# Part of a layer norm's statistics moved from DVE to Pool, and the last tile's tail in halves, in a two-layer linear-attention kernel

## The chip, the cores and the metric

The kernel runs on one core of a Trainium2 chip. The metric is the device time of one execution in microseconds (us), and lower is better. Times are medians of several executions, with the lowest and the highest in brackets. A profile is one execution of its own and its span is about 1.7 us shorter than the execution's time (392.7 against 394.39 us for the kernel before).

The engines are PE (matrix multiplication), PEld (PE's weight loads, which overlap its matmuls), DVE (vector), ACT (scalar), POOL (GpSimd) and SP (which only issues transfers here).

## The reference

Two equal layers, each of a linear attention block and a gated MLP, both behind a layer norm and with a residual. Here x is 1 x 2048 x 512, there are 32 heads of 16, F is 1376 and everything is bf16.

```python
def _layernorm(x, axis=-1, eps=1e-5):
    m = jnp.mean(x, axis=axis, keepdims=True)
    v = jnp.var(x, axis=axis, keepdims=True)
    return (x - m) / jnp.sqrt(v + eps)

def _A_ref(x, wqkv, w_phi, wo):            # shortened
    q, k, v = split_heads(x @ wqkv)
    pq, pk = q @ w_phi, k @ w_phi           # for each head
    phi_q = concat([softmax(pq), softmax(-pq)])
    phi_k = concat([softmax(pk), softmax(-pk)])
    kv, z = sum_s(phi_k outer v), sum_s(phi_k)
    return merge_heads(phi_q @ kv / (phi_q @ z + 1e-6)) @ wo

def _B_ref(x, W_gate, W_up, W_down):       # shortened
    gate = x @ W_gate
    return (relu(gate) * (x @ W_up)) @ W_down

x = x + _A_ref(_layernorm(x), ...);  x = x + _B_ref(_layernorm(x), ...)
x = x + _A_ref(_layernorm(x), ...);  x = x + _B_ref(_layernorm(x), ...)
```

## The kernel before

The sequence is cut into 16 tiles of 128 rows. The kernel isn't written as streams of instructions. It records operations, each with an engine, the resources that it reads and writes, and a duration from a table. A list scheduler then chooses one order for all of them. It runs forward and backward passes over modelled start times, replays each order found with durations varied by up to 8%, and keeps the order with the shortest modelled span. The order is then emitted as one in-order stream per engine, with semaphores for the dependences.

```python
class Program:                                            # cut
    def schedule(self):
        ...
        noise = [[rng.uniform(0.92, 1.08) for _ in ops] for _ in range(self.TRIALS)]
        best = None
        for weight in self.ORDER_WEIGHTS:                 # 4 weights
            prio = [weight * o.idx - rank[o.idx] - o.boost for o in ops]
            for _ in range(self.PASSES):                  # 12 passes
                start, finish, order = self._forward(prio)
                span = self._replay(order, noise)
                if best is None or span < best[0]:
                    best = (span, start, finish, order)
                prio = [t - o.boost for t, o in zip(self._backward(start, finish), ops)]

    def _forward(self, prio):
        ...
            if o.is_dma:
                q_free = max(st + self.DMA_FIXED * 0.35, q_free) + o.dma_bytes / self.DMA_BW
                finish[i] = q_free + self.DMA_FIXED * 0.65
            else:
                finish[i] = st + o.dur
```

The first layer norm ("L0") runs its statistics in batches of four tiles. For tiles 4 to 15 the odd tiles are applied on ACT, the even ones on DVE, and a DMA transposes each result for PE:

```python
    def ln_stats(self, ts, tag):
        ...
        for t in ts:
            op("dve", bn_stats(stats6[t] <- x_sb[t]), 685, f"{tag} stats {t}")         # two halves: count, mean, count x variance
            op("dve", bn_aggr(mv[t] <- stats6[t]),    172, f"{tag} aggr {t}")          # mean, variance
        op("pool", tensor_scalar(rv1[t0:t1] <- mv[..., 1:2] + EPS_LN), 225 + 4 * n, f"{tag} rv1 {t0}")
        op("pool", tensor_tensor(rstd[t0:t1] <- rv1 pow mhalf),        550 + 20 * n, f"{tag} rstd {t0}")

    def ln(self, t, tag, on_act=False, ...):
        ...
        if on_act:
            op("pool", nmr[t] <- mv[t, 0] * rstd[t] * -1.0, 280, f"{tag} nmr {t}")
            op("act", activation(ytile <- x_sb[t], Identity, scale=rstd[t], bias=nmr[t]), 825, f"{tag} apply {t}")
        else:
            op("dve", tensor_scalar(ytile <- (x_sb[t] - mv[t, 0]) * rstd[t]), 407, f"{tag} apply {t}")
        ...
        self.dma_tr(yT[:, :, t * 128:(t + 1) * 128] <- ytile, f"{tag} tr {t}")
```

These are shortened: the lambdas and resource lists are left out. In the same stage, the keys of the attention are normalised: a sum on DVE ("Zk"), a reciprocal on DVE ("rZk") and a multiplication of 128 x 1024 on Pool ("phik"), for tiles 14 and 15 half on Pool and half on DVE.

The tail is the down projection of tile 15 in the last MLP, its residual add and its store:

```python
    def glu_down(self, t, ring, tag):
        bank = next(ring)
        for fc in range(NFC):                                       # 11 matmuls of 512 columns
            op("pe", matmul(pb[bank] += hT[fc].T @ Wd[fc]), 216, f"{tag} down {t} {fc}")
        op("dve", x_sb[t] <- x_sb[t] + pb[bank], 685, f"{tag} resid {t}")

    def store(self, t):
        self.dma("sp", out[t] <- x_sb[t], ..., 131072, f"store {t}")
```

The softmax here doesn't subtract the row's maximum and nothing guards it: scores larger than these inputs give would overflow.

## Time and profile before

| | before |
|---|---|
| time | 394.07 us (393.86 to 394.39, 3 runs) |
| span of the profile | 392.7 us |
| PE busy | 377.3 us (96%), 2277 matmul records for 2320 weight loads |
| PE clock granted | full in every slice |
| last key normalisation on Pool ends | 53.2 us |

First come lines of the profile page of the kernel before: the busy times (in brackets the share of the span, then the number of instructions), and the shares by engine of the chain of work that ended last.

```profile
PE 377.3 (96%) x2277; PEld 206.9 (53%) x2320; DVE 267.4 (68%) x554; ACT 207.1 (53%) x389; POOL 166.4 (42%) x272
...
PE 84%; DVE 5%; POOL 4%; DMA 2%; ACT 2%; issue 2%; SPq 0%; DVEq 0%; ACTq 0%; POOLq 0%
```

PE bounds the kernel. Note the two counts: each matmul of this kernel has a weight load of its own, so 43 matmul records are missing from this trace.

Next is the table by stretches of the kernel before (some stretches are left out): start and end, then sum and mean of the stretch's length, then the busy time of each engine with the number of instructions.

```profile
core 0: us, PE busy (x) PEld busy (x) DVE busy (x) ACT busy (x) POOL busy (x), PEclk, DMA share, GB/s
10.00:20.00 10.00, 8.93 (x49) 4.47 (x49) 9.67 (x28) 8.43 (x16) 3.60 (x8) 1.00 0.83 211
20.00:30.00 10.00, 8.83 (x65) 4.94 (x65) 10.00 (x14) 9.73 (x14) 8.89 (x8) 1.00 0.38 73
30.00:40.00 10.00, 9.62 (x61) 5.01 (x62) 9.36 (x13) 8.08 (x11) 10.00 (x6) 1.00 0.40 80
80.00:240.00 160.00, 159.11 (x921) 84.92 (x935) 117.55 (x225) 70.00 (x138) 71.56 (x109) 1.00 0.17 33
262.00:280.00 18.00, 16.80 (x131) 12.34 (x133) 14.36 (x40) 9.52 (x27) 9.37 (x23) 1.00 0.29 60
```

From 10 to 40 us DVE and ACT are busy 80% of the time or more, Pool nearly all of it from 20 us on, and PE has gaps. In the middle PE is nearly full. But read 80 to 240 us with the counts: there are 921 matmuls for 935 loads, and fourteen missing matmuls account for the missing 0.9 us. The gap in 262 to 280 us, of 1.2 us, is another matter, since only two records are missing there.

Two more views of the kernel before, by time (start, duration, engine, line, operation, output<-inputs; in square brackets the idle time before it and what ended it), show the stage that the change edits. DVE:

```profile
21.45 2.04 DVE L564 TENSOR_SCALAR ytile<-x_sb,mv,rstd 128x512 bf16<-128x512 bf16 x1
23.41 0.54 DVE L601 RECIPROCAL rZk<-Zk 128x64 f32<-128x64 f32 x1
```

Pool:

```profile
21.42 1.93 POOL L604 TENSOR_TENSOR expk<-expk,rZk 128x1024 bf16<-128x1024 bf16 x1
...
24.11 1.93 POOL L604 TENSOR_TENSOR expk<-expk,rZk 128x1024 bf16<-128x1024 bf16 x1 [0.17 <-DVE rZk L601]
26.69 1.94 POOL L604 TENSOR_TENSOR expk<-expk,rZk 128x1024 bf16<-128x1024 bf16 x1 [0.65 <-DVE rZk L601]
```

The DVE apply at 21.45 (tile 6) lasted 2.04 us instead of about 0.4: it lay over the whole of Pool's first normalisation. That pushed the reciprocal behind it to 23.41, and Pool then twice waited for reciprocals.

The tail of the kernel before, on DVE:

```profile
388.83 0.69 DVE L754 TENSOR_TENSOR x_sb<-x_sb,ps 128x512 bf16<-128x512 bf16 x1 [3.29 <-PE ps L752]
389.69 0.69 DVE L754 TENSOR_TENSOR x_sb<-x_sb,ps 128x512 bf16<-128x512 bf16 x1 [0.18 <-PE ps L752]
```

### The profile page before, as it was taken

Reading aid. Unit: us, or ns where it says so; the run is one execution under the profiler, and the core shown is the slowest. Engines: PE = TensorE matmul, PEld = TensorE weight load, DVE = VectorE, ACT = ScalarE, POOL = GpSimd, SP = SyncE. Lnnn points to the kernel's source line nnn. Section 1 sums busy time; section 2 is a strip of 40 time slices with the busy share of each in tenths; the row PEclk is TensorE's granted clock in tenths of the full one; section 3 lists DMA queues with packets and bytes.
Section 4 is the critical chain, followed back from the end, with each engine's and each line's share of the span. In section 5 each row is a group of like instructions: output and inputs, shape, how many; then the busy total and the mean of one; then the engine's idle time right before and its main releaser. Section 6 shows DMA issues by size and latency. Waiting matters only on the chain.

```text
span 392.7 us, 6311 instructions
## 1 busy us (share of the span) xinstructions
PE 377.3 (96%) x2277; PEld 206.9 (53%) x2320; DVE 267.4 (68%) x554; ACT 207.1 (53%) x389; POOL 166.4 (42%) x272
## 2 busy tenths in 40 slices
PE   5889999999999999999999999989999999999996
PEld 3445564677644444444444467467774454444442
DVE  4999878777757899857747867877875666222122
ACT  5898659744624413532553484975564462453350
POOL 5389945642623463363334552574444253000000
PEclk9999999999999999999999999999999999999999
DMA  6833672322211322401000110242323132100001
GB/s 182 220 69 79 200 276 43 67 53 43 42 40 27 43 53 46 85 7 29 13 13 2 27 29 2 48 61 53 76 54 61 27 56 53 42 14 13 15 27 53
DMA packets 61519, 23.01 MB, mean 59 GB/s; under 512 B 53456, under 2 KB 60464, under 8 KB 61488
## 3 DMA queue, kind: packets, MB, share of 16 engines
q1 hardware_dynamic: 60912, 22.08, 24.8%
q10 hardware_dynamic: 576, 0.52, 0.5%
q8 instruction: 18, 0.29, 0.3%
q14 instruction: 13, 0.11, 0.1%
HBM read 7.91 MB, written 2.10 MB: 25 GB/s over the span
## 4 chain that ended last, share of the span: by engine, by line
PE 84%; DVE 5%; POOL 4%; DMA 2%; ACT 2%; issue 2%; SPq 0%; DVEq 0%; ACTq 0%; POOLq 0%
PE ps L728 39%; PE ps L752 19%; PE ps L587 7%; PE ps L707 6%; PE ps L660 5%; PE ps L676 4%; POOL expk L604 3%; DVE stats L547 2%; PE ps L633 2%; PE ps L618 2%; DMA yT<-ytile 1%; DMA x_sb<-in_A_x_dram 1%; POOL rstd L552 1%; DVE ytile L564 1%; ACT expq L663 1%
## 5 line engine op out<-in xcount | busy, mean ns | idle before, releaser
L728 PE MATMUL ps<-yT,Wg 128*128 128x512 bf16 (+3 forms) x435 | 125.9, 336 | 2.0 <-ACT numbf L366 1.1
L728 PE MATMUL ps<-yT,Wu 128*128 128x512 bf16 (+3 forms) x436 | 124.2, 336 | 0.4
L730 ACT ACTIVATE gate_sb<-ps 128x512 bf16<-128x512 f32 (+3 forms) x110 | 56.2, 512 | 108.7 <-PE ps L728 103.2
L752 PE MATMUL ps<-Wd,hT 128*128 128x512 bf16 (+1 forms) x340 | 104.0, 379 | 0.6
L604 POOL TENSOR_TENSOR expk<-expk,rZk 128x1024 bf16<-128x1024 bf16 (+1 forms) x32 | 59.6, 1878 | 30.9 <-DVE rZk L601 21.6
L728 PEld LDWEIGHTS ps<-yT,Wg 128*128 128x128 bf16 (+1 forms) x440 | 43.7, 100 | 34.4 <-issue 1.5
L728 PEld LDWEIGHTS ps<-yT,Wu 128*128 128x128 bf16 (+1 forms) x440 | 43.7, 100 | 33.4 <-ACT expk L735 0.8
L752 PEld LDWEIGHTS ps<-Wd,hT 128*128 128x128 bf16 (+1 forms) x352 | 34.1, 98 | 37.3 <-DVE x_sb L754 0.7
L737 DVE TENSOR_TENSOR hT<-gate_sb,expk 128x512 bf16<-128x512 bf16 (+3 forms) x73 | 28.7, 393 | 31.0 <-ACT expk L735 30.2
L547 DVE BATCH_NORM_STATS2 stats<-x_sb 128x6 f32<-128x512 bf16 x64 | 42.1, 675 | 5.0 <-DMA x_sb<-in_A_x_dram 4.7
L599 DVE TENSOR_REDUCE Zk<-expk 128x64 f32<-128x1024 bf16 x32 | 38.0, 1197 | 10.1 <-ACT expk L590 8.4
L366 ACT ACTIVATE numbf<-ps 128x432 bf16<-128x432 f32 x64 | 32.9, 538 | 17.7 <-PE ps L676 17.4
L701 POOL TENSOR_TENSOR osb<-tsc 128x512 bf16<-128x512 bf16 x28 | 32.7, 1168 | 21.3 <-DVE tsc L696 18.2
L707 PE MATMUL ps<-wo_p,oT 128*128 128x512 bf16 x122 | 38.7, 379 | 0.2
L551 POOL TENSOR_SCALAR rv<-mv 128x1 f32<-128x1 f32 (+1 forms) x55 | 12.3, 229 | 61.0 <-DVE mv L548 60.8
L735 ACT ACTIVATE expk<-ps 128x512 bf16<-128x512 f32 (+3 forms) x73 | 36.2, 495 | 0.6 <-PE ps L728 0.4
L754 DVE TENSOR_TENSOR x_sb<-x_sb,ps 128x512 bf16<-128x512 bf16 x32 | 21.7, 682 | 20.8 <-PE ps L752 20.6
L663 ACT ACTIVATE expq<-ps 128x1024 bf16<-128x1024 f32 (+1 forms) x40 | 32.3, 865 | 6.1 <-PE ps L660 5.8
L676 PE MATMUL ps<-kvbd,expq 128*128 128x144 bf16 x256 | 34.6, 226 | 0.4 <-DVE kvbd L649 0.2
L660 PE MATMUL ps<-yT,Wqp 128*128 128x512 bf16 x121 | 33.6, 379 | 1.2 <-ACT expq L663 1.0
L740 DVE TENSOR_TENSOR hT<-gate_sb,ps 128x512 bf16<-128x512 bf16 (+2 forms) x37 | 22.6, 612 | 17.7 <-PE ps L728 15.7
L552 POOL TENSOR_TENSOR rstd<-rv,mhalf 128x1 f32<-128x1 f32 (+1 forms) x55 | 33.1, 607 | 3.1
(62 smaller groups left out, 428.9 us busy)
## 6 DMA issues: line engine op xcount, KB each, us to landing
out_dram<-x_sb SPq DMA_DIRECT2D x16, 128.0 KB, 1.7
x_sb<-in_A_x_dram SPq DMA_DIRECT2D x3, 512.0 KB, 6.2
Wg<-in_B_W_gate_dram SPq DMA_DIRECT2D x4, 344.0 KB, 4.2
Wu<-in_B_W_up_dram SPq DMA_DIRECT2D x4, 344.0 KB, 6.6
Wd<-in_B_W_down_dram SPq DMA_DIRECT2D x5, 256.0 KB, 7.3
yT<-ytile SPq DMA_TRANSPOSE x60, 2.4
hT<-in_A_wqkv_dram ACTq DMA_DIRECT2D x4, 128.0 KB, 3.2
x_sb<-in_A_x_dram SPq DMA_DIRECT2D x4, 128.0 KB, 3.8
```

The costliest lines, as they stand in the source:

```text
L547: op("dve", (lambda t: lambda e: e.bn_stats(k.stats6[:, t, :], k.x_sb[:, t, :]))(t), [r("x", t)], [r("st", t)], 685, f"{tag} stats {t}")
L552: op("pool", lambda e: e.tensor_tensor(k.rstd[:, t0:t1, :], k.rv1[:, t0:t1, :], k.mhalf[:, 0:n], ALU.pow), [r("rv1", t) for t in ts] + [r( ...
L599: op("dve", lambda e: e.tensor_reduce(k.Zk[:, zb, :], k.expk[:, t, :, :].rearrange("p s (h f) -> p (s h) f", f=16), AX.X, ALU.add), [r("ex ...
L604: op(eng, (lambda s0, s1: lambda e: e.tensor_tensor(k.expk[:, t, s0:s1, :].rearrange("p s (h f) -> p (s h) f", f=16), k.expk[:, t, s0:s1, ...
L660: op("pe", (lambda c, ic, bank: lambda e: e.matmul(k.pb[bank][:], k.Wqp[:, ic, c * 128:(c + 1) * 128], k.yT[:, ic, st * 512:(st + 1) * 512 ...
L663: op("act", (lambda c0, s, b0: lambda e: e.activation(k.expq[:, st, c0:c0 + w, s, :], k.ps[:, b0:b0 + w, :], ACT.Exp, scale=(1.0 - 2.0 * s ...
L676: op("pe", (lambda s, c, j, g0, bank: lambda e: e.matmul(k.pb[bank][:, j * GW:(j + 1) * GW], k.expq[:, st, c, s, tt * 128:(tt + 1) * 128], ...
L707: op("pe", (lambda c, bank: lambda e: e.matmul(k.pb[bank][:], k.oT[:, ob, c, :], k.wo_p[:, c, :], start=(c == 0), stop=(c == NC - 1)))(c, ...
L728: op("pe", (lambda bank, W, ic, fc, Mf: lambda e: e.matmul(k.pb[bank][0:Mf, 0:n], W[:, ic, fc * 128:fc * 128 + Mf], k.yT[:, ic, c0:c0 + n] ...
L730: op("act", (lambda Mf, gb, gs: lambda e: e.activation(k.gate_sb[0:Mf, gs, 0:n], k.pb[gb][0:Mf, 0:n], ACT.Relu))(Mf, gb, gs), [self.RP[gb] ...
L735: op("act", (lambda Mf, ub, tu: lambda e: e.activation(k.expk[0:Mf, tu, 0, 0:n], k.pb[ub][0:Mf, 0:n], ACT.Copy))(Mf, ub, tu), [self.RP[ub] ...
L752: op("pe", (lambda fc, Kf, u, c0: lambda e: e.matmul(k.pb[bank][:], k.hT[0:Kf, u, c0:c0 + 128], k.Wd[0:Kf, fc, :], start=(fc == 0), stop=( ...
```

## The change

The intent has two parts. First, the mean and variance of tiles 8 to 15 of the first layer norm are no longer aggregated on DVE, tile by tile. Pool merges the half statistics of four tiles at once with small operations, and makes the bias for four tiles in one. All applies of tiles 4 to 15 then have the form x * rstd + bias. Second, the down projection of the very last tile is done in two halves of 256 columns, so that only half of the residual add and half of the store follow the last matmul.

```diff
@@ ln_stats (cut)
-            op("dve", ... bn_aggr ..., 172, f"{tag} aggr {t}")
+            if tag != "L0" or ts[0] < 8:
+                op("dve", ... bn_aggr ..., 172, f"{tag} aggr {t}")
+        if tag == "L0" and ts[0] >= 8:
+            return self.aggr_pool(ts, tag)
@@ new (resource lists cut; d = 225 + 4 * n)
+    def aggr_pool(self, ts, tag):
+        op("pool", df <- s6[:, :, 0, 1:2] - s6[:, :, 1, 1:2], d, f"{tag} agdif {t0}")
+        op("pool", sm <- s6[:, :, 0, 1:3] + s6[:, :, 1, 1:3], d, f"{tag} agsum {t0}")
+        op("pool", df <- df * df, d, f"{tag} agsq {t0}")
+        op("pool", sm <- sm * [-0.5, 1 / D], d, f"{tag} agmul {t0}")
+        op("pool", df <- df * 0.25 + EPS_LN, d, f"{tag} agv {t0}")
+        op("pool", rv1 <- df + sm[1], d, f"{tag} rv1 {t0}")
+        op("pool", rstd <- rv1 pow mhalf, 550 + 20 * n, f"{tag} rstd {t0}")
+        op("pool", nmr <- sm[0] * rstd, d, f"{tag} nmr {t0}")
@@ ln (cut)
+        if tag == "L0" and t > 3:
+            if t < 8:
+                op("pool", nmr[t] <- mv[t, 0] * rstd[t] * -1.0, 280, f"{tag} nmr {t}")
+            ...                  # DVE: x * rstd + nmr, 407; ACT as before, 825
@@ glu_down (cut)
-               ..., 216, f"{tag} down {t} {fc}")
+    def glu_down(self, t, ring, tag, halves=1):
+        w = 512 // halves
+        for m in range(halves):
+            bank = next(ring)
+            ...                  # matmul into pb[bank][:, m0:m1] from Wd[:, fc, m0:m1]
+               ..., 0.42 * w + 1, f"{tag} down {t} {fc}")
+            ...                  # residual of the half, 150 + 1.045 * w
@@ store (cut)
+        for m in range(halves):
+            self.dma("sp" if m == 0 else "act", ..., 131072 // halves, f"store {t}")
@@ steps_B
-                    out.append(lambda t=t: self.glu_down(t, dring, B))
+                    out.append(lambda t=t: self.glu_down(t, dring, B, 1 + (last and t == NT - 1)))
```

One side effect: the table's durations of all full down projections turn from 216 to 216.04 and of their residual adds from 685 to 685.04.

## The prediction

> **What bounds the kernel now.** TensorE. On the page PE is busy 377.3 of 392.7 us (96%), and the chain of waits is 84% PE. The table by stretches puts the missing PE time at the two ends: idle 4.4 us in 0–10 us, 1.1 in 10–20, 1.2 in 20–30, 0.4 in 30–40, 0.05 in 40–50, 1.15 in 50–60, about 0.8 in 60–80, and 3.1 in the last 14.7 us. From 80 to 378 us it idles only some 3.3 us of 298. So the change, which touches only the first layer norm (until about 36 us) and the last tile, can move the time by one or two microseconds at most; a gain of 2% (7.9 us) isn't there to be had.
>
> **First layer norm.** Between 10 and 36 us DVE is 94–100% busy and carries the chain (statistics, aggregation, reciprocal, apply), which ends in a wait of PE for a transposed tile at 31 us. The change takes eight aggregations off DVE. One lasts 172 ns, but four in a row add only 0.28 us to the chain, so DVE gains about 0.56 us, not the 1.4 us that the durations suggest. The applies stay on their engines (309–412 ns on DVE).
>
> Pool gets six small operations (0.23–0.24 us each, with 0.07 us between dependent ones) in place of one before each power (1.03 us), and one batched bias operation in place of two; tiles 4 to 7 get two biases more (0.27 us each). That is about +1.4 us of Pool per batch, and each batch's applies can start some 1.5 us later, since all of them now wait for the bias. Batch 8–11 can use Pool idle time (2.6 us before 17.47, 0.67 before 20.11). Batch 12–15 can't: Pool runs the key normalisations from 21.42 to 53.25 us with about 1.2 us idle, and their end releases the last accumulation at 53.3. Unless the scheduler puts a normalisation earlier, that end moves back by about 1 us. The whole order is computed anew, so this may be avoided: the reciprocal that the first normalisation needs ran at 19.93, though its sum was done at 14.2.
>
> One DVE apply took 2.04 us instead of 0.41: it lies wholly over Pool's first normalisation (21.42–23.35). The Trainium skill, "SBUF — State Buffer", section "Who interferes with whom", says that DVE in a two-port mode and GpSimd hold the shared port pair exclusively, so one blocks the other for a whole instruction. The trace agrees with that, and it is 1.6 us on the chain; a shifted order can remove or repeat it.
>
> Net for this part: −0.4 us, uncertain by 1.3.
>
> **Tail.** The last residual add (0.69 us) and then a 1.7 us store follow the last matmul alone. In halves the exposed add is about 0.42 us, with the store of half the bytes on another queue: −0.3 us. PE's down time shouldn't grow: 256-wide matmuls in the page's gate/up groups go at 0.109 us each, half of 0.216.
>
> **Prediction.** 393.4 us, 8 in 10 between 391.9 and 395.1. Faster by over 2%: 0.01; within 2%: 0.98; slower by over 2%: 0.01.
>
> **What would show it.** Right: the aggregation line falls from 64 to 56 executions; DVE's statistics of tiles 8–15 run back to back; about 16 small Pool operations appear before 24 us; from the last matmul to the end it is 0.3 us shorter; PE busy unchanged; the last key normalisation ends within 1.5 us of 53.25. Wrong: that end moved by more than 2 us, or PE idle time between 80 and 378 us changed by over 1 us.
>
> **What would make it wrong.** The recomputed order changing the PE-bound middle; more or fewer DVE applies blocked by Pool; Pool's normalisations starting much earlier or later; half-row stores landing more slowly.

## The result, and the profile after

The kernel after takes 391.80 us (391.07 to 392.33, 4 runs), against 394.23 us (393.86 to 394.43, 4 runs) for the kernel before. The ratio is 0.9938, with a 95% interval from 0.9919 to 0.9957. Here and below, ratios are the mean time of one kernel's runs over that of the other's in the same rounds, so they are not quite the ratio of the medians quoted. The gain is real: the change was measured three times in all, at 0.9938, 0.9939 and 0.9949.

The page of the kernel after, the lines that answer to those of before:

```profile
PE 379.4 (97%) x2331; PEld 208.0 (53%) x2331; DVE 272.0 (70%) x547; ACT 206.6 (53%) x389; POOL 168.5 (43%) x284
...
PE 88%; POOL 4%; ACT 3%; DMA 2%; DVE 1%; issue 1%; ACTq 0%; POOLq 0%
```

This trace is complete: 2331 matmuls and 2331 loads, the 11 more being the halves. So PE's busy time, 379.4 against 377.3 us, says nothing of more work; most of the difference is the 43 missing records. What did move is DVE's share of the chain, from 5% to 1%.

The table by stretches of the kernel after, cut in the same way:

```profile
core 0: us, PE busy (x) PEld busy (x) DVE busy (x) ACT busy (x) POOL busy (x), PEclk, DMA share, GB/s
10.00:20.00 10.00, 9.05 (x50) 4.50 (x49) 9.42 (x21) 8.88 (x18) 4.60 (x14) 1.00 0.88 223
20.00:30.00 10.00, 9.69 (x63) 4.86 (x62) 10.00 (x14) 9.36 (x13) 9.75 (x13) 1.00 0.32 64
30.00:40.00 10.00, 10.00 (x75) 5.65 (x73) 10.00 (x13) 8.75 (x11) 10.00 (x7) 1.00 0.32 71
80.00:240.00 160.00, 160.00 (x942) 85.20 (x941) 116.24 (x225) 68.72 (x136) 70.13 (x108) 1.00 0.17 32
262.00:280.00 18.00, 18.00 (x147) 13.35 (x146) 15.32 (x37) 10.01 (x30) 8.62 (x19) 1.00 0.29 52
```

PE is fuller in 20 to 40 us, where the change edits. It is also full in 262 to 280 us, where the change edits nothing.

**A measure that missing records don't spoil.** The weight loads are complete in both traces and each starts right before its matmul. So for the n-th weight load I subtract from its start the time that all matmuls before it take at full rate, by the median interval of their width in the traces (about 0.216 us for 512 columns, 0.2158 in the sums below, 0.109 for 256, 0.0625 for 144, 0.057 for 129). What is left is the time that PE has lost so far. This is worked out from the traces, one execution of each kernel:

| lost by (us of the span) | 10 | 60 | 80 | 242 | 262 | 280 | 376 | after that, to the end |
|---|---|---|---|---|---|---|---|---|
| before | 7.33 | 12.66 | 13.93 | 14.04 | 15.19 | 16.27 | 16.24 | 376.43 |
| after | 7.11 | 11.50 | 12.87 | 13.08 | 14.23 | 14.27 | 14.40 | 375.86 |
| after, second profile | 7.35 | 11.51 | 12.88 | 13.08 | 14.24 | 14.48 | 14.62 | |
| after, third profile | 7.32 | 11.00 | 12.23 | 12.49 | 13.59 | 13.69 | 13.67 | |

The last column is the span less the loss by 376 us: all matmul work plus the tail. So the 2.41 us between the two spans divide into about 1.0 us that are won early and still held at 262 us (1.16 by 60 us), 0.9 won from 262 to 376 us, nearly all of it by 280, and 0.57 in the tail. The three profiles of the changed kernel agree within 0.5 us in the first stage. Five kept traces in which the first stage is that of before (before itself and four experiments below) have lost 11.9 to 12.7 us by 60 us, against 11.0 to 11.5. So the gain there is real, but a difference of under 0.8 us between two single traces says nothing.

**The first stage.** The DVE of the kernel after:

```profile
19.62 0.40 DVE L592 TENSOR_SCALAR ytile<-x_sb,rstd,nmr 128x512 bf16<-128x512 bf16 x1
19.94 0.54 DVE L631 RECIPROCAL rZk<-Zk 128x64 f32<-128x64 f32 x1
20.40 2.28 DVE L629 TENSOR_REDUCE Zk<-expk 128x64 f32<-128x1024 bf16 x2
22.60 0.54 DVE L631 RECIPROCAL rZk<-Zk 128x64 f32<-128x64 f32 x1
...
26.41 1.92 DVE L592 TENSOR_SCALAR ytile<-x_sb,rstd,nmr 128x512 bf16<-128x512 bf16 x1
```

And its Pool:

```profile
17.42 0.20 POOL L570 TENSOR_TENSOR agg<-stats 128x4 f32<-128x4 f32 x1 [1.51 <-DVE stats L551]
...
18.74 1.02 POOL L576 TENSOR_TENSOR rstd<-rv,mhalf 128x4 f32<-128x4 f32 x1
19.84 0.24 POOL L577 TENSOR_TENSOR nmr<-agg,rstd 128x4 f32<-128x4 f32 x1
21.07 1.93 POOL L634 TENSOR_TENSOR expk<-expk,rZk 128x1024 bf16<-128x1024 bf16 x1
...
24.21 1.93 POOL L634 TENSOR_TENSOR expk<-expk,rZk 128x1024 bf16<-128x1024 bf16 x1
26.25 1.93 POOL L634 TENSOR_TENSOR expk<-expk,rZk 128x1024 bf16<-128x1024 bf16 x1
```

The apply of tile 6 now runs at 19.62, before Pool's first normalisation, and lasts 0.40 us. The sums for two key normalisations come straight after, so Pool has its reciprocals early: it is hardly ever idle from 17.42 us until its last normalisation ends at 52.00 us (53.24 before). Blocked applies are not gone; the one at 26.41 lasts 1.92 us, but by then reciprocals are in stock. The lock itself is what the Trainium skill, "SBUF — State Buffer", section "Who interferes with whom", describes: in its two-port modes DVE takes the port pair that it shares with GpSimd for the whole instruction, and whoever comes second waits. This trace agrees too: 0.40 us free against 1.92 to 2.04 us over a 1.93 us Pool instruction. The profile doesn't say in which mode an instruction ran.

The merge chain of tiles 8 to 11 on Pool, from 17.42 to 20.08, lasts 2.66 us. The four operations in its place in the kernel before (17.47 to 19.43) lasted 1.96 us. So it costs 0.7 us more, half of the predicted 1.4: each small operation shows 0.20 us, and independent ones start every 0.16 us.

**262 to 280 us.** The waits of PE's weight loads in this stretch, in the kernel before (out, line <- what ended the wait: total us, times, longest):

```profile
PEld ps L707 <- DMA oT<-osb: 1.1, 1, 1.1
```

And in the kernel after:

```profile
PEld ps L706 <- ACT numbf L366: 0.3, 1, 0.3
PEld ps L737 <- issue: 0.2, 1, 0.2
PEld ps L737 <- DMA oT<-osb: 0.2, 1, 0.2
```

In the kernel before, PE stood for 1.1 us, until 263.94, in front of the first output-projection matmul of tile 4 in the second layer, whose transposed input came late. The view of that transposing line in the kernel before, 250 to 270 us, with the times from issue to landing:

```profile
L704 SPq DMA_TRANSPOSE oT<-osb x5: 1189/1191/1486, 251.4 to 266.8; - x5
...
DMA to landing us min/median/max: 2.4/2.5/4.3
```

Three of the five landed within 2.5 us of their issue; this one took 4.3. PE's matmuls run strictly in program order (the Trainium skill, "TensorE: Matmul & The Clock Gate", section "Step-by-step: what each phase is for": only weight loads are pulled ahead, the matmuls stay in order), so every matmul behind it waited too, ready or not. The trace agrees: no matmul ran in those 1.1 us. In the five other kept traces with the old order in this stretch, the transpose of tile 4 landed 3.5 to 4.4 us after its issue and the wait was 0.4 to 1.3 us. In the kernel after, one transpose is as late (tile 5's, 4.0 us) but its matmul stands further back in PE's stream, and PE waits 0.2 us.

**The tail.** DVE and the last store of the kernel after:

```profile
385.39 0.69 DVE L787 TENSOR_TENSOR x_sb<-x_sb,ps 128x512 bf16<-128x512 bf16 x1 [0.40 <-PE ps L785]
387.36 0.86 DVE L787 TENSOR_TENSOR x_sb<-x_sb,ps 128x256 bf16<-128x256 bf16 x2 [1.28 <-PE ps L785]
...
388.25 0.35 ACTq L794 DMA_DIRECT2D out_dram<-x_sb  x1
```

The two half adds span 0.86 us together and only the second, about 0.42 us, lies behind the last matmul, where 0.69 us lay before. From the modelled end of the last matmul to the end of the trace it is 2.50 us, against 3.02 before. Tile 14's add starts 2 us before tile 15's here; in the kernel before the two start within 0.9 us of each other.

### The profile page after: what moved, and what is told of

Same layout as the page of the kernel before. It is cut to its first block, busy times and chain, and to the rows that moved or that the text cites. A ratio compares the mean times of both kernels' runs of the same rounds, so it can differ in the third digit from the quotient of the medians.

```text
span 390.3 us, 6397 instructions
## 1 busy us (share of the span) xinstructions
PE 379.4 (97%) x2331; PEld 208.0 (53%) x2331; DVE 272.0 (70%) x547; ACT 206.6 (53%) x389; POOL 168.5 (43%) x284
## 4 chain that ended last, share of the span: by engine, by line
PE 88%; POOL 4%; ACT 3%; DMA 2%; DVE 1%; issue 1%; ACTq 0%; POOLq 0%
PE ps L758 39%; PE ps L785 19%; PE ps L617 7%; PE ps L737 7%; PE ps L690 6%; PE ps L706 4%; PE ps L663 3%; PE ps L648 2%; POOL expk L634 2%; ACT expq L693 2%; DVE stats L551 1%; DMA x_sb<-in_A_x_dram 1%; DMA hT<-in_A_wqkv_dram 1%; ACT expk L620 1%; POOL rstd L576 1%
## 5 line engine op out<-in xcount | busy, mean ns | idle before, releaser
L758 PE MATMUL ps<-yT,Wg 128*128 128x512 bf16 (+3 forms) x440 | 130.1, 337 | 0.5 <-DMA yT<-ytile 0.2
L758 PE MATMUL ps<-yT,Wu 128*128 128x512 bf16 (+3 forms) x440 | 129.6, 336 | 0.0
L785 PE MATMUL ps<-Wd,hT 128*128 128x512 bf16 (+2 forms) x363 | 106.8, 373 | 0.0
L767 DVE TENSOR_TENSOR hT<-gate_sb,expk 128x512 bf16<-128x512 bf16 (+3 forms) x73 | 29.8, 409 | 37.9 <-ACT expk L765 33.0
L785 PEld LDWEIGHTS ps<-Wd,hT 128*128 128x128 bf16 (+1 forms) x363 | 35.3, 98 | 36.6 <-DVE x_sb L787 0.6
L737 PE MATMUL ps<-wo_p,oT 128*128 128x512 bf16 x128 | 39.8, 379 | 0.0
L620 ACT ACTIVATE expk<-ps 128x512 bf16<-128x512 f32 x44 | 23.9, 598 | 21.5 <-PE ps L617 21.2
L690 PE MATMUL ps<-yT,Wqp 128*128 128x512 bf16 x128 | 34.6, 379 | 0.6 <-ACT expq L693 0.5
L787 DVE TENSOR_TENSOR x_sb<-x_sb,ps 128x512 bf16<-128x512 bf16 (+1 forms) x33 | 22.0, 669 | 18.8 <-PE ps L785 18.4
L559 POOL TENSOR_TENSOR rstd<-rv,mhalf 128x1 f32<-128x1 f32 (+1 forms) x53 | 31.9, 607 | 2.9
```

Source lines behind the costliest of these rows:

```text
L690: op("pe", (lambda c, ic, bank: lambda e: e.matmul(k.pb[bank][:], k.Wqp[:, ic, c * 128:(c + 1) * 128], k.yT[:, ic, st * 512:(st + 1) * 512 ...
L737: op("pe", (lambda c, bank: lambda e: e.matmul(k.pb[bank][:], k.oT[:, ob, c, :], k.wo_p[:, c, :], start=(c == 0), stop=(c == NC - 1)))(c, ...
L758: op("pe", (lambda bank, W, ic, fc, Mf: lambda e: e.matmul(k.pb[bank][0:Mf, 0:n], W[:, ic, fc * 128:fc * 128 + Mf], k.yT[:, ic, c0:c0 + n] ...
L785: op("pe", (lambda fc, Kf, u, c0, bank, m0, m1: lambda e: e.matmul(k.pb[bank][:, m0:m1], k.hT[0:Kf, u, c0:c0 + 128], k.Wd[0:Kf, fc, m0:m1] ...
```

## The experiments

**The theories.** All agree that PE bounds the kernel.

1. The instructions theory: the gain comes from the edited instructions, from fewer on DVE and from a shorter tail. It expects a gain when the edits are put into the old order, and none from the order by itself.
2. The order theory: most of the gain comes from the new order that the scheduler drew. It expects most of the gain with the old instructions in the new order, and little with the new instructions in the old one.
3. Two sub-theories name what in the order matters. One is the blocked apply of tile 6 in the first stage. The other is the matmul that stood in front of a late transpose in the second layer. A later form, theory L, claims that the scheduler's orders are good or bad because its table knows no late transposes, so that a table which expects them would cure it.

The expectations below were written before the runs, some with short names for these theories.

**The means.** One source holds both parts of the change behind flags (merge, halves). The diffs of the experiments are shortened and their names changed for reading; in the sources the flags are AGG and TAIL. It can compute the place of each named operation in the order of another combination and emit its own operations in those places:

```diff
+    def places(self, merge, halves):          # the order of that combination, by the operations' names
+        prog = self.once(merge, halves); prog.schedule()
+        return {o.name: float(j) for j, o in enumerate(sorted(prog.ops, key=lambda o: (o.start, o.idx)))}
+    def plan(self):
+        at = self.places(*ORDER); self.moves(at)   # moves: the single edits of an experiment
+        prog = self.once(MERGE, HALVES); prog._derive_deps()
+        for o in prog.ops:                    # never before what it depends on
+            o.start = max(at.get(o.name, 0.0), 0.001 + max(start of its dependences))
```

An operation that the other order doesn't have is put directly behind what it depends on; restored aggregations go behind their batch's last statistics. Every kernel below gave a correct result. "Before" is the kernel before, run on the same chip in the same rounds.

### First group: instructions against order

Merge alone, in the order of before (before: 394.31 us in this group, 393.66 to 394.94, 11 runs).

```diff
+    MERGE, HALVES, ORDER = 1, 0, (0, 0)
```

> The statistics merge on Pool alone, with every instruction left in the order of the kernel before (new ones put where their inputs are ready). Theory O (the recomputed order carries the gain): within 0.4 us of before, 393.8 to 394.6, and TensorE's lost time up to 80 us stays at 13.9 us. Rival W (the eight aggregations taken off VectorE carry the gain of the first stage, in any order): 0.8 to 1.1 us faster than before, and the last key normalisation ends about 1 us earlier.

Measured: 394.27 us (392.82 to 394.73), ratio 0.9989 (0.9973 to 1.0005), -0.40 us by the means. The interval includes no change.

Halves alone, in the order of before.

```diff
+    MERGE, HALVES, ORDER = 0, 1, (0, 0)
```

> The tail in halves alone, everything else in the order of before. Both theories: 0.3 to 0.6 us faster (residual add 0.69 to 0.42 us, store of half the bytes about 0.2 us shorter), trace before 385 us as before. If the halves cost TensorE time instead, it is no faster than before.

Measured: 394.50 us (393.75 to 395.82), ratio 1.0004 (0.9988 to 1.002), +0.20 us by the means. No gain, where 0.3 to 0.6 us were expected. The trace shows a flaw of this experiment. Here are its weight loads at the end:

```profile
385.17 2.17 PEld L786 LDWEIGHTS ps<-Wd,hT 128*128 128x128 bf16 x15 [0.32 <-DVE x_sb L788]
...
388.40 1.43 PEld L786 LDWEIGHTS ps<-Wd,hT 128*128 128x128 bf16 x14 [1.06 <-DVE x_sb L788]
```

The second half goes to the PSUM bank of tile 14. In the old order tile 14 ends so late that its residual add frees the bank only at 388.35, and PE stands for 1.06 us by its weight loads (0.67 us by its matmuls, whose recorded ends are modelled). So the halves need an order in which tile 14 ends earlier; this run doesn't tell their worth.

Old instructions, in the order of the changed kernel.

```diff
+    MERGE, HALVES, ORDER = 0, 0, (1, 1)
```

> The instructions of before (no merge, no halves) in the order of the changed kernel. Theory O: 1.3 us or more faster than before (392.9 or less), with the TensorE wait of 1.1 us near 264 us gone and the first stage about 0.5 to 1 us shorter. Rival W: the first stage is as before, so at most the 0.9 us of the second layer is won: 393.3 or more.

Measured: 393.05 us (392.61 to 393.42), ratio 0.9964 (0.9951 to 0.9977), -1.40 us by the means. Not one edited instruction is in this kernel, and it has more than half of the gain. PE's loss by 376 us is 14.87 (before 16.24), so the measure agrees: -1.37 us. By 60 us it is 11.85 (before 12.66) and from 262 to 280 us 0.37 (before 1.08); of these two, the first lies within the scatter of single traces.

Old instructions, order drawn anew: only the two table values of the side effect.

```diff
-               ..., 216, f"{tag} down {t} {fc}")
+               ..., 216.04, f"{tag} down {t} {fc}")
-           ..., 685, f"{tag} resid {t}")
+           ..., 685.04, f"{tag} resid {t}")
```

> The instructions of before, with two durations in the scheduler's own table changed by 0.04 ns, as the change does in passing; so only the order is drawn again. Theory O: the time moves by 0.5 to 1.5 us in either direction although no instruction differs. Rival W: within 0.3 us of before.

Measured: 393.79 us (392.53 to 394.21), ratio 0.998 (0.9965 to 0.9995), -0.76 us by the means. Changing two numbers that describe durations by 0.04 ns, with no instruction touched, moves the time by about as much as the predicted worth of the change.

The four together make the instructions theory fail: it expected nothing from the order by itself, and the order by itself brought 1.40 us (0.9 to 1.9 by the interval). What the halves are worth is still open at this point.

### Second group: which moves in the order

The first kernel moves one DVE operation: the apply of tile 6 goes ahead of the first reciprocal, in the order of before (before: 394.6 us, 393.22 to 395.3, 11 runs).

```diff
+        at["L0 apply 6"] = at["A0 rZk 0"] - 0.5
```

> The kernel before with one VectorE instruction moved: the apply of tile 6 in the first layer norm goes ahead of the first reciprocal, as the changed kernel has it, instead of behind the first normalisation on Pool, where it took 2.04 us. If the order of the first stage carries its gain: that apply takes 0.3 to 0.45 us, Pool no longer waits for the second and third reciprocal (0.17 and 0.65 us), the last key normalisation ends 0.6 to 1.2 us earlier, and the time is 0.5 to 1.1 us below before. If VectorE's work carries it: another apply is blocked instead and the time stays within 0.3 us.

Measured: 393.99 us (393.6 to 395.0), ratio 0.9995 (0.9976 to 1.0014), -0.30 us by the means. The move itself did what it should; its DVE has the apply unblocked:

```profile
20.19 0.38 DVE L595 TENSOR_SCALAR ytile<-x_sb,mv,rstd 128x512 bf16<-128x512 bf16 x1
```

But another apply, at 25.27, now took 1.03 us, and Pool's last normalisation ended at 52.88 us, only 0.4 earlier instead of 0.6 to 1.2. In the five traces whose first stage is that of before it ends between 52.49 and 53.88, so even this is no clear difference. Whether the single blocked apply is worth 0.3 us or nothing stays inconclusive; 1.6 us lies outside the interval.

The second moves one PE operation: the first of the four output-projection matmuls of tile 4, second layer, goes back by about 4 us to its three companions.

```diff
+        at["A2 wo 4 0"] = at["A2 wo 4 1"] - 0.5
```

> The kernel before with one matmul moved: the first of the four output projection matmuls of tile 4 in the second attention layer goes next to the other three, about 4 us later. If the gain near 264 us is that TensorE no longer stands before a late transpose: the 1.1 us wait goes, TensorE's lost time between 262 and 280 us falls from 1.1 to under 0.3 us, and the time is 0.8 to 1.1 us below before. If the tiles themselves come too late: the wait moves to the next matmuls and the gain is under 0.3 us.

Measured: 393.77 us (392.31 to 394.0), ratio 0.9979 (0.9961 to 0.9997), -0.90 us by the means. Between 262 and 280 us PE lost 0.05 us (before 1.08), and its weight loads have no wait at all there. One matmul of 2320 in another place is worth 0.9 us (0.1 to 1.5 by the interval). This explains the gain far from any edited instruction.

Merge alone, with the order drawn for it.

```diff
+    MERGE, HALVES, ORDER = 1, 0, None
```

> The statistics merge without the tail in halves, its order drawn anew. Theory O: as fast as its order is lucky, 392.0 to 393.8, and not tied to the merge, which in the old order was worth 0.04 us of median. Rival W: about 1 us below before and no more, all of it before 60 us.

Measured: 396.84 us (395.61 to 398.74), ratio 1.007 (1.0042 to 1.0097), +2.66 us by the means. That is outside both expectations. Two of its six runs had a granted clock of 0.994 and 0.996 (398.67 and 398.74 us); the four at full clock took 395.61 to 397.43 us, still 1.85 us above before by the means. So the same merge that measured -0.40 in the old order loses in its own. PE's weight loads wait for transposes for some 6.9 us in this trace.

Halves in the old order, mended: all down projections of tile 14 before those of tile 15.

```diff
+        for fc in range(NFC):
+            at[f"B3 down 15 {fc}"] = at["B3 down 14 10"] + 0.01 * (fc + 1)
```

> The tail in halves in the order of before, but with the down matmuls of tile 14 all ahead of those of tile 15, so that the second half's PSUM bank is free in time. If the bank wait of 0.65 us ate the gain of the tail: 0.4 to 0.8 us below before. If the halves are worth nothing in themselves: within 0.3 us of before.

Measured: 394.96 us (393.65 to 395.38), ratio 1.0009 (0.999 to 1.0027). Again no gain, and again a fault of mine: the residual add and the store of the first half still stood behind those of the second.

### Third group: the change once more, and its own order broken

The changed kernel again, all code as in the change (before: 394.24 us, 393.78 to 395.28, 11 runs).

> The changed kernel once more, on the chip of the three runs beside it. Both theories: 2.0 to 2.7 us below before.

Measured: 391.98 us (391.67 to 392.28, 5 runs), ratio 0.9939 (0.9925 to 0.9952), -2.37 us by the means. The result repeats.

Halves alone, in the order of the changed kernel.

```diff
+    MERGE, HALVES, ORDER = 0, 1, (1, 1)
```

> The changed kernel without the merge (aggregations back on VectorE), in the changed kernel's order, tail in halves. Its difference to the changed kernel is the merge in that order, its difference to the run of the old instructions in the new order is the tail. If the order carries most: 1.5 to 2.0 us below before, 0.3 to 0.6 above the changed kernel. If the merge carries most: no more than 1.2 below before.

Measured: 392.38 us (392.06 to 393.69), ratio 0.9956 (0.9941 to 0.9971), -1.73 us by the means.

Every instruction of the changed kernel, with the two table values put back.

```diff
-               ..., 0.42 * w + 1, f"{tag} down {t} {fc}")
+               ..., 216 if halves == 1 else 0.42 * w + 1, f"{tag} down {t} {fc}")
-           ..., 150 + 1.045 * w, f"{tag} resid {t}")
+           ..., 685 if halves == 1 else 150 + 1.045 * w, f"{tag} resid {t}")
```

> The instructions of the changed kernel, every one, with the scheduler's two durations of the down projection put back by 0.04 ns to what they were before; only the order is drawn again. Theory O: the time leaves that of the changed kernel by 0.5 us or more, in either direction. Rival W: within 0.3 us of the changed kernel.

Measured: 395.47 us (395.04 to 400.87), ratio 1.005 (1.001 to 1.009), +1.98 us by the means. The highest run had a granted clock of 0.991 (without it the mean is +1.08 us); the other five were at full clock, and their lowest is still above every run of the changed kernel. So the same instructions cost 391.98 or 395.47 us, by whether the table says 216.04 or 216. The waits of PE's weight loads from 20 to 376 us, in this kernel:

```profile
PEld ps L738 <- DMA oT<-osb: 3.5, 3, 2.3
PEld ps L649 <- DMA yT<-ytile: 2.2, 2, 1.4
PEld ps L618 <- DMA yT<-ytile: 1.5, 1, 1.5
```

And those of the kernel before, in the same stretch:

```profile
PEld ps L707 <- DMA oT<-osb: 1.4, 2, 1.1
PEld ps L618 <- DMA yT<-ytile: 0.8, 1, 0.8
```

That is 7.2 us of waits for transposes against 2.2. The longest, 2.3 us at 96.2, is again for a transpose that landed 4.3 us after its issue. PE's loss by 376 us is 18.64 us, against 14.40 in the changed kernel: the whole difference is PE's waits. The scheduler saw none of this. Its modelled span of this order is 391.4 us and of the changed kernel's order 391.7: it holds the slower one for the better. Building the other kernels gives its spans for them too: 393.3 us for the order of before, 393.0 for its redraw and 392.0 for the merge alone. The model ranks that order well ahead of before, and it measured 2.66 us behind.

Halves in the old order, mended twice.

```diff
         for fc in range(NFC):
             at[f"B3 down 15 {fc}"] = at["B3 down 14 10"] + 0.01 * (fc + 1)
+        at["B3 resid 15"] = at["B3 resid 14"] + 0.0005
+        at["store 15"] = at["store 14"] + 0.0005
```

> As the second tail experiment, which left the residual add and the store of the first half behind those of the second half; here they go ahead, as the change has it. 0.4 to 0.7 us below before by the trace from the last down matmul to the end (1.3 us plus store before, about 0.85 us plus store here); by the runs 0.3 or more.

Measured: 393.78 us (393.1 to 394.57), ratio 0.9985 (0.997 to 1.0), -0.58 us by the means. The halves gain in the old order too now, though the interval just reaches no change. The trace agrees with a gain: the span less PE's loss by 376 us falls from 376.43 to 376.07.

### Fourth group: a table that expects late transposes

The prediction had missed, and the question left was what makes an order good. These runs let the model land every transpose later, and draw a new order from that (before: 394.22 us, 393.53 to 395.21, 11 runs).

```diff
+        o.lag = 1600.0                        # on transposes; 0 on all else
-                finish[i] = q_free + self.DMA_FIXED * 0.65
+                finish[i] = q_free + self.DMA_FIXED * 0.65 + o.lag
```

Changed instructions, lag of 1.6 us:

> The instructions of the changed kernel, order drawn with every transpose taken to land 1.6 us later than the table has it (with this the draw no longer depends on the 0.04 ns: both tables give the same order). Theory L: TensorE's waits for transposes from 20 us to 376 us are under 1 us in sum (7.2 in the unlucky draw, 0.2 in the changed kernel), and the time is 391.0 to 392.6. Rival S: as the first stage gets no shorter, 393 or more.

Measured: 395.93 us (394.56 to 397.91), ratio 1.0035 (1.0016 to 1.0053), +1.76 us by the means. Its profiled execution, also its slowest, had a granted clock of 0.996; without it the mean is +1.38 us, and the five at full clock took 394.56 to 396.43 us. In the profiled one the weight loads wait elsewhere, from 20 to 376 us:

```profile
PEld ps L709 <- ACT numbf L367: 3.9, 10, 0.7
PEld ps L651 <- issue: 3.2, 6, 1.8
PEld ps L693 <- ACT expq L696: 1.5, 2, 0.7
```

The waits for transposes are gone, and waits for ACT and for PE's own issue have taken their place.

Changed instructions, lag of 0.8 us:

> The same with 0.8 us. Theory L: waits for transposes under 2.5 us, time 391.0 to 393.2, far under the 395.5 of the unlucky draw. Rival S: scatter as without the lag, 391.5 to 396.

Measured: 393.87 us (393.39 to 394.22), ratio 0.9989 (0.9975 to 1.0002), -0.43 us by the means. That is worse than theory L expected, though only 1.5 us of waits for transposes are left.

Instructions of before, lag of 1.6 us:

> The instructions of before with the order drawn under the 1.6 us lag. Theory L: waits for transposes fall from 2.2 us to under 1 us and the time is 1 to 2 us below before, 392.3 to 393.4, though nothing of the change is in it. Rival S: within 0.6 us of before.

Measured: 396.04 us (394.12 to 397.34), ratio 1.0038 (1.0013 to 1.0064), +1.53 us by the means. Three of its six runs had a granted clock of 0.995 to 0.996 (396.7 to 397.34 us); the three at full clock took 394.12 to 395.39 us. So at full clock it is some 0.35 us behind before, by the median 394.57.

Theory L falls as a cure: a table that expects late transposes everywhere gives worse orders, or at best equal ones. Only some transposes are late, and the slack that the model reserves for all is taken from other places.

The fourth kernel of this group builds the gain by hand, without the merge: the order of before, with the two single moves of the second group and the twice mended halves.

```diff
+    MERGE, HALVES, ORDER = 0, 1, (0, 0)
+        at["L0 apply 6"] = at["A0 rZk 0"] - 0.5
+        at["A2 wo 4 0"] = at["A2 wo 4 1"] - 0.5
+        ...                                  # and the mended halves as above
```

> The order of before with the two single moves (apply of tile 6 early, first output projection matmul of tile 4 late) and the tail in halves as last mended; no merge. If the moves add: 1.3 to 2.0 us below before (0.3 to 0.5, 0.8 to 1.0 and 0.4 to 0.6). If they do not add, because a later wait takes up what an earlier one gives: under 1 us.

Measured: 392.93 us (392.09 to 393.44), ratio 0.996 (0.9945 to 0.9976), -1.54 us by the means. PE's loss by 376 us is 14.32, as in the changed kernel (14.40). Two moved operations and the halves give about two thirds of the result, with no statistics moved to Pool. (The profiled execution was its fastest, 392.09 us, so the loss flatters it a little.) The parts alone (-0.30, -0.90, -0.58) would add up to -1.78.

### Fifth group: two more edits of the changed kernel

The trace of the changed kernel still has a blocked apply (tile 10, 1.92 us at 26.41). This kernel puts it right behind tile 8's with its transpose, and lets DVE take half of tile 13's key normalisation, in the order of the changed kernel (before: 393.91 us, 393.01 to 394.85, 11 runs).

```diff
+        at["L0 apply 10"] = at["L0 apply 8"] + 0.3
+        at["L0 tr 10"] = at["L0 tr 11"] - 0.3
+        at["A0 phik 13 1"] = at["A0 phik 14 1"] - 0.3
-        parts = [("pool", 0, 2)] if t < NT - 2 else [("pool", 0, 1), ("dve", 1, 2)]
+        parts = [("pool", 0, 2)] if t < NT - (3 if tag == "A0" else 2) else [("pool", 0, 1), ("dve", 1, 2)]
```

> The changed kernel in its own order with two edits: the apply of tile 10 goes right behind that of tile 8, where Pool runs only small operations (it took 1.92 us behind a normalisation), and VectorE takes half of the key normalisation of tile 13 as it already does of 14 and 15. If Pool ends the first stage: Pool's last normalisation ends 0.3 to 0.6 us earlier and the time is 0.2 to 0.6 us below the changed kernel beside it. If VectorE is the limit too: its half normalisations, blocked by Pool, end later and the time is equal or above.

Measured: 391.34 us (391.14 to 392.28), ratio 0.9937 (0.9921 to 0.9952), -2.47 us by the means. The apply takes 0.41 us, Pool's last normalisation ends at 50.72 and PE's loss by 376 us is 13.14.

The changed kernel, a third time, as the partner of that run:

> The changed kernel again, beside the run above: 2.0 to 2.6 us below before.

Measured: 391.98 us (391.01 to 392.82), ratio 0.9949 (0.993 to 0.9968), -1.98 us by the means. The edited kernel is 0.64 us ahead by the medians and 0.49 by the means, but the intervals overlap and the lowest run belongs to the changed kernel. It is the fastest kernel that I measured; that it beats the changed one isn't proven.

## Why the prediction was right or wrong

The predicted time was 393.4 us, from 391.9 to 395.1. The measured 391.80 us lies 0.1 us outside. The sign and the class ("within 2%") were right, and the gain was 2.43 us against a predicted 0.67.

**The step that failed** is this one: "So the change, which touches only the first layer norm (until about 36 us) and the last tile, can move the time by one or two microseconds at most". The change touches only those instructions, but it draws the order of all of them anew: about 850 of PE's 2320 matmuls changed their place relative to the others (the redraw of before alone moved 32). The prediction entered this only as an uncertainty of the first stage and as a warning. In the sum, the term "new order" had the size zero. The runs put these sizes in its place, each by the means against before, run beside it:

| what was added | total | step |
|---|---|---|
| order of the changed kernel, old instructions | -1.40 | -1.40 |
| with the halves | -1.73 | -0.33 |
| with the merge: the change | -2.37 | -0.64 |

The first row was run on another chip than the other two. The step of the halves, -0.33, is smaller than the intervals. The traces show it better: from the modelled end of the last matmul to the end it is 3.01 us without the halves and 2.49 with them, in the same order.

The intervals of the last two ratios (0.9941 to 0.9971 and 0.9925 to 0.9952) overlap slightly, and in the old order the merge's -0.40 includes zero. So the merge's worth isn't shown, beyond that it is some tenths of a microsecond in these two orders. The traces don't place its gain either: PE's loss by 60 us is 11.31 us without it and 11.00 to 11.51 with it, in the same order.

What is shown is that the order by itself moves the time, in both directions: -1.40 with no edit; and with all edits, 3.5 us between two orders, one of which the scheduler's model wrongly prefers. That it carries more than the edits is likely, but the intervals overlap: the edits add about 1.0 us in the new order (-2.37 less -1.40), and singly in the old order about as much in sum (-0.40 and -0.58). The gain of 2.4 us belongs to this edit together with this draw. That the draw was a good one was luck: nothing in the edit asks for it, and two other draws with the merge in them measured 1.98 and 2.66 us behind before.

Point by point:

- Merge, predicted -0.4 net: measured -0.40 (old order) and -0.64 (new order). The size fits, within intervals that don't prove it. The reasoning behind it did not hold (see Pool's last normalisation below), so the fit is partly luck.
- Halves, predicted -0.3: measured -0.33 (new order) and -0.58 (mended old order), and 0.5 us by the traces of the end. Right in kind, and rather too small. The unforeseen part is a condition: the second half needs tile 14's PSUM bank, so tile 14 must be out of the way, or 1.06 us are lost.
- "That end moves back by about 1 us" (Pool's last normalisation): wrong in sign. It came 1.24 us earlier, while Pool's idle time (0.17 + 0.65 + 0.26 + 0.44 us in the kernel before) vanished and the merge chain grew by 0.7 us and not 1.4. This goes with the order and not with the merge: with the merge in the old order it ends at 53.20, and without the merge in the new order at 52.20 and 51.81 (halves). The hint was in the prediction ("a shifted order can remove or repeat it", and the reciprocal that could have run earlier), but it wasn't counted.
- The blocked apply as "1.6 us on the chain": wrong. Moving it alone gained 0.30 us by the means, in an interval that includes zero and ends before 1 us.
- "From 80 to 378 us it idles only some 3.3 us of 298": too high by about 1 us, which was missing matmul records (2277 of 2320). The other 2.3 us were really lost, and the prediction gave no part of them to the new order. By the weight loads PE lost 0.1 us from 80 to 242, 1.15 from 242 to 262, 1.08 from 262 to 280, and nothing after. The 1.08 us was a single wait that the waits view shows by name, and it could have been priced as something that a new order may remove or add.
- "A gain of 2% isn't there to be had": right as far as the runs go. After the first 10 us PE lost 16.24 - 7.33 = 8.9 us in the kernel before, so 7.9 us would have been nearly all of it; the best kernel that I ran still lost 13.14 - 7.35 = 5.8 us.
- Of the signs for being wrong that the prediction named, one came: PE's idle time between 80 us and 376 or 378 us fell from 3.3 to 0.4 us by the table by stretches (from 2.3 to 1.5 by the weight loads).
- The things to look for came as predicted: statistics of tiles 8 to 15 back to back but for one apply, some sixteen small Pool operations, a shorter end, and aggregations down from 64 to 56. The groups of before and of after:

```profile
L548 DVE BATCH_NORM_AGGREGATE mv<-stats x64: 123/173/183, 5.1 to 333.1; 128x2 f32<-128x6 f32 x64
```

```profile
L553 DVE BATCH_NORM_AGGREGATE mv<-stats x56: 115/175/183, 5.3 to 332.0; 128x2 f32<-128x6 f32 x56
```

**What stays open.** Why particular transposes land late was tested by no run, but the kept traces hold a strong lead. Of the 92 transposes issued from SP that move a tile, 16 in the kernel before and 13 in the changed one landed more than 2.7 us after issue, seven and six of them 3.8 us or more. Some places in the sequence of SP's transfers (counted from 0: 50, 76 and 121) are late in all four traces that I compared (before, two of the changed kernel, and the changed kernel redrawn), at place 121 even though another tile stands there in the last one. The view of the DMA queues of the kernel before also lists packets of a kind that it calls instruction (queue, kind: packets, MB, share of the 16 engines):

```profile
q8 instruction: 18, 0.29, 0.3%
q14 instruction: 13, 0.11, 0.1%
```

Each of these packets carries 16 KB (q8) or 8 KB (q14) and took 0.3 to 1.7 us over all kept traces; the median of the other packets of the kernel before is 0.018 us. In the kernel before, such a packet was in flight within 2.4 us of issue for all 16 late transposes and for 5 of the other 76. In the changed kernel it was 13 of 13 and 11 of 79, and over all 20 kept traces 293 of 294 and 167 of 1546. The transpose that PE waited for until 263.94 was issued at 259.63, and one of 16 KB ran from 260.77 to 262.34; that of the wait at 96.2 in the changed kernel redrawn was issued at 91.8, and one ran from 93.83 to 95.07. That these packets make the transposes late is therefore likely. It isn't shown, as no run moved one.

## What to carry to other kernels

When a scheduler or a compiler orders the program, an edit is two changes: the instructions and a new draw of the order. Measure them apart, by putting the old instructions into the new order and the new ones into the old, and redraw once with nothing changed to see how much a draw is worth; here that was -0.8 us in one redraw and +3.5 us in another, against edits of a few tenths. In a program bound by an in-order engine, look in the trace for the single instruction in front of a late input, because moving it by a few microseconds can be worth as much as the edit itself.

## What the Trainium skill lacked or had wrong

- "DMA: Bandwidth & Descriptors", section "DMA Transpose (X-bar)": it gives constraints but no latency for a small transpose from SBUF to SBUF, no word on its scatter, and none on DMA packets of the kind "instruction", one of which was in flight soon after the issue of nearly every late one (293 of 294). Here one of 128 x 512 bf16 lands about 2.4 us after issue, but in the kernel before 16 of 92 took over 2.7 us and seven of these 3.9 to 5.1 us. Where the matmul stood right behind a late one, PE waited 1.1 us (kernel before) to 2.3 us (changed kernel redrawn).
- "TensorE: Matmul & The Clock Gate", section "Back-to-back issue gap": it says that a stream of weight load and matmul pairs sustains about 131 ns per matmul of 512 columns, and that the 216 ns of a single one over-counts. Here every matmul has its own weight load and the median interval of 512 columns is 216 ns (109 ns for 256), so the page's formula for a single matmul fits and its figure for the stream doesn't.
- "Perfetto Trace Analysis", section "Tensor Engine Instruction (MATMUL, LD_WEIGHTS)": it says that a matmul's end time is a model. It doesn't say that whole matmul records can be missing: here 43 of 2320, which looked like 2 us of idle PE. The weight loads were complete and served as the clock.
